# Hedgehog attention into an ELU MLP on one core: MLP chunks cut along the batches, a ring for the transposed activations, some PSUM copies on the other engine, and a new written-out order

## The chip, the core and the metric

The kernel runs on one core of a Trainium2 chip. The core has a matrix engine (TensorE; "PE" in the profile, its weight loads "PEld"), a vector engine (VectorE, "DVE"), an activation engine (ScalarE, "ACT"), a general-purpose engine (GpSimd, "POOL") and a queue engine (SyncE, "SP"). Each engine works through its own instruction list in order and waits on semaphores for the others. The metric is the device time of one execution in microseconds (us); lower is better.

## What is computed

Inputs are q, k and v of shape 8 x 8 x 576 x 64 (batch, head, position, head dimension), a feature matrix w_phi of 64 x 128, and two MLP weights of 512 x 2048 and 2048 x 512. All are float32.

```python
def phi(x):
    proj = einsum('bhsd,df->bhsf', x, w_phi)
    proj = proj - max(abs(proj), axis=-1, keepdims=True)
    return concatenate([exp(proj), exp(-proj)], axis=-1)
q_p, k_p = phi(q), phi(k)
kv  = einsum('bhsf,bhsd->bhfd', k_p, v)
z   = sum(k_p, axis=2)
num = einsum('bhsf,bhfd->bhsd', q_p, kv)
den = einsum('bhsf,bhf->bhs', q_p, z)[..., None] + 1e-06
x   = (num / den).transpose(0, 2, 1, 3).reshape(4608, 512)
h   = x @ w_in
g   = where(h > 0, h, exp(min(h, 0)) - 1)
out = g @ w_out                      # 4608 x 512, float32
```

So a linear attention with an exponential feature map feeds an MLP with the ELU function. The attention has no softmax over positions; its per-row maximum is taken over the 128 features.

## The kernel before

**Attention, by groups.** Four heads (two pairs) of one batch make a group; there are NG = 16 groups, two for each batch, numbered n. Positions are cut into nine slots of 64, and a tile of 128 rows holds one slot of two heads, or two slots of one head. A group goes through these steps, each named by a letter in the order string:

- e, f, g (L189): load k, q and v of a batch by DMAs that the POOL queue issues and that cast to bf16. h and i load w_in (two halves) and w_out the same way.
- j/k and l/m (L207, L219): PE transposes and VectorE copies of k and q for groups 0 to 3. n and o (L225): DMA transposes on the SP queue for groups 4 to 15.
- A, B, C (L233, L247, L254): k times w_phi, two exponentials on ScalarE (128 x 768 each), row maxima on VectorE. D, E, F: the exponential of the maxima, and v scaled by it on POOL (L275).
- M, N (L287, L303): q times w_phi and its row maxima. O (L317): the maxima split into two bf16 parts, 128 x 18, by a cast and a subtraction; P (L333): a PE transpose of them; Q (L338): its copy from PSUM (128 x 128).
- S, T (L343, L390): the projection of q with the maximum subtracted by a second matmul, and two exponentials.
- U, V (L401, L417): k_p times v, accumulated over the nine slots, and its copy from PSUM (128 x 520).
- W, X (L430, L448): q_p times kv, and the division on VectorE. The result goes, transposed, into `xT_sb`, by PE and copies (Y, Z) for groups 0 and 1 and by SP's DMA transposes (z, L490) for the others.

**MLP, by chunks.** The 4608 tokens are cut into nine chunks of 512 columns of `xT_sb`, one constant tile that holds all tokens. p (L507): for each of 16 blocks of d_ff, four matmuls of 512 columns (in chunk 0, two halves of 256 columns). q, r, s (L519 to L533): exponential on ScalarE, clamp on POOL, and the ELU result on VectorE. t (L535): the second product, four times four matmuls for each of four token tiles; u (L546): its copy from PSUM on ScalarE (128 x 512, float32), v (L550): two stores. In `xT_sb` the columns of a batch pair stand as 512 (slots 0 to 7 of the first batch), 128 (slot 8 of both), 512 (slots 0 to 7 of the second). The nine chunks therefore run across batch boundaries.

**What sets the order.** Nothing is scheduled by a framework: all pools stand in one manual schedule, and the string `ORDER` lists 1737 steps. A letter calls the next step of its kind, and a digit names the PSUM bank that the step writes:

```python
for letter, bank in re.findall(r"([A-Za-z])(\d?)", "".join(ORDER.split())):
    fn, args = queues[letter]
    fn(*next(args), **({"bank": int(bank)} if bank else {}))
```

Each engine's instruction list is the order of the string with the other engines' steps left out. A step is on a fixed engine; only `m_split` (O) chooses, POOL for groups below `PE_TRANSPOSED` = 4 and VectorE otherwise:

```python
eng = nc.gpsimd if n < PE_TRANSPOSED else nc.vector
```

The MLP steps of a chunk are interleaved with the attention steps of later groups.

Of the kernel before, what the change touches and what calls it, by code (L numbers as in the profile page):

```python
# [18 lines left out]
eabefegcj7dfkA0gj7BfkBeA2CA4hBl7gl6Bmj1mj0hBCM6iBkkA2DCBFEl1NDA4Bl0EmBOCFP1BEA6QBmS2CEM0CTU4eNDB  # L19
EUTOEM6VM0DP3NW4EQNM6S2NM0OTFENU6TXP1FOUQS2VP5Y4Tj1ZS6QTl0W4mTS2kTj0XTW6TkS4XA0Tj3BY2ZA6Tkl2Bp3m  # L20
Y5BCqBZrA0p4sCM2qp5rNM6qDrBNp3l2sqp7BmrsqM4rp6NFp2qsqrp5srp4CqOqrP7l3srW0sgQmp6sEj7XqS2DTrEkM0p5
NY7qTsrS0sFp4EZTsM2M6TNp5EqNS0qrp3Trp2sOsTA6fp4CqU0qrrUBssVqA2Bp5rW0sBP7p6Xqnt4qrBrsp1QCp5zqp7qr
sp0qrszW2DsrqFsS5rEp1sTXp7qp0Trfsp3qA1rtBesqp7ECoqp6qtDrBrsp5rzsqEp0sqS1qztTrrsFTsp7EU5uS1qrUrTs
A3Vt0TCtsBW1oW5BXp7A3qtCzrtsBXzt7BnM1A5M3NBtuCztDFNEM0BztNgM2uvt6ODENP7M0nM4QNES2tTNFTfS0S4TEA2t
CTp7TTU0UBA4VtBCp1qorBW2sqp0vBOXrp7quP5p4rzQsDqFW2sqrzp6XrA0qEp5szBsp3rqCvp7rqseBp4vsrqp6DsrqS0s
rM2Tp5NFEqp7sqrp3qrsTp4rsqsM0qA5rt2CEp7NBrtsBsM0qS5NtrTEsTS0U3oTA5UCTtVBt7OnBP4W0QuS3XvW5TtDXzTE
tztfFA0EuzS2M4Bt6NTztCTS4BM2otDTEtzTFA0Eut7CntNgBA4BM2CtNtBBA0OU2CUDuP6p5VQM2qM6Np4rNEp3qBsW6rqp
2sBrp5XqFeW0qsrzS6DXrp4TEzTp3sqEsvM0S6Np2TFnEqS0Tp5rqrsU6qzrUsTrp4TzOsp3qVorA0qsA6p2Brsvsp5qCP4r
p3qQCBrp4qsW0qrst2DXBEp5BFsW0zrqtEszXS6rtTvsM0A3NtBnTt5CztDBFEM0S6zNM3TtENTU0guA3S6UTotVBvt2BtTC
p1OA3qW6urp0XBP5tBQztqCzS5uA3t7DCTEntsDBFtrBEsW1TtXEA3uM5ep0NzBEp7Cqvp6rBFsM1qp5NqrM3qrS0Np2Trsf  # L30
# [15 lines left out]
def kernel(  # L46
# [34 lines left out]

    consts = ctx.enter_context(tc.tile_pool(name="consts", bufs=1))
# [5 lines left out]
    moep = ctx.enter_context(tc.tile_pool(name="moep", bufs=2))  # L88
    epool = ctx.enter_context(tc.tile_pool(name="epool", bufs=4))
# [24 lines left out]
    xT_sb = consts.tile([P, N_CT, NTOK], BF16)  # L114
    FULL = 4 * P

    def full_col(b):
        return (b // 2) * 2 * S + (b % 2) * (FULL + P)

    def mixed_col(b):  # L120
        return (b // 2) * 2 * S + FULL + (b % 2) * D

    def out_rows(tile_index):
        bp, t = divmod(tile_index, 9)
        rows = []
        for half in range(2):
            if t == 4:
                b, s = 2 * bp + half, 8
            else:
                b, t4 = (2 * bp, t) if t < 4 else (2 * bp + 1, t - 5)  # L130
                s = 4 * (t4 // 2) + t4 % 2 + 2 * half
            rows.append(
                out[b * S:(b + 1) * S, :].rearrange("(p s) c -> s p c", s=NS)[s]
            )
        return rows
# [11 lines left out]
    PIECES = (((0, 4), (4, 7), (7, 9)), ((0, 3), (3, 6), (6, 9)))  # L147
    TILES = (
# [56 lines left out]


# [12 lines left out]
    def t_copy(name, n, j0, j1):  # L219
        nc.vector.tensor_copy(  # L220
            get((name + "T", n), new_t(name))[:, j0:j1, :],
            st["tr", name, n, j0][:, 0:j1 - j0, :],
        )

    def t_dma(name, n):  # L225
        nat = st[name, n // 2][:, 2 * (n % 2):2 * (n % 2) + 2]
        nc.sync.dma_start_transpose(
            out=get((name + "T", n), new_t(name)),
            in_=nat.rearrange("p r s d -> p (r s d)"),
        )  # L230
# [56 lines left out]
    def m_mm(n, c, bank=None):  # L287
        own = min(n // FIRST, 1)
# [14 lines left out]
    def m_max(n, c):  # L303
        p0, p1 = PIECES[min(n // FIRST, 1)][c]
# [12 lines left out]
    def m_split(n, part):  # L317
# [5 lines left out]
        if n < FIRST and part == 0:  # L323
            mq, eng = st["mq0", n], nc.vector
        else:
            mq = st["mq", n][:, :, p[0]:p[1]]
            eng = nc.gpsimd if n < PE_TRANSPOSED else nc.vector
# [10 lines left out]
    def m_copy(n, part):  # L338
        st["mT", n] = tpool.tile([P, 1, P], BF16, name="mT")
        nc.vector.tensor_copy(st["mT", n], st["trm", n][:, 0:1, :])  # L340


    def q_mm(n, c, bank=None):  # L343
# [3 lines left out]
        qT, mT = st["qT", n], st["mT", n]  # L347
# [17 lines left out]
        for x in range(max(len(r) for r in runs)):  # L365
            for par in range(2):
                if x >= len(runs[par]):
# [6 lines left out]
                    qT[rows, i:i + m, :].rearrange("p i (h t) -> p h i t", h=2),  # L374
                    start=(x == 0),
                    stop=False,
                )
        for j in range(w):
            for par in range(2):
# [4 lines left out]
                    mT[rows, 0, :],  # L384
# [32 lines left out]
    def kv_copy(n):  # L417
        st["kv", n] = work.tile([P, 2, 2, 2, D + 1], BF16, name="kv_sb")
        nc.vector.tensor_copy(
# [10 lines left out]
    def x_mm(n, part, bank=None):  # L430
        Eq, kv_sb = st["Eq", n], st["kv", n]
        parts = x_parts(n, part)
# [30 lines left out]

    def x_pe(n, part, bank=None):
# [8 lines left out]
    def x_copy(n, part):  # L473
# [3 lines left out]
        c0 = full_col(b) + part * 2 * P  # L477
        nc.vector.tensor_copy(
            xT_sb[:, 2 * g:2 * g + 2, c0:c0 + 2 * P].rearrange(
# [4 lines left out]
        if part == 1:  # L484
            nc.vector.tensor_copy(
                xT_sb[:, 2 * g:2 * g + 2, mixed_col(b):mixed_col(b) + D],
                tr[:, :, 2, D:P],
            )

    def x_dma(n, pr, mixed):  # L490
        b, g = divmod(n, 2)
        xp, ct = st["xp", n, pr], 2 * g + pr
        if not mixed:
            nc.sync.dma_start_transpose(
                out=xT_sb[:, ct, full_col(b):full_col(b) + FULL].rearrange(
# [4 lines left out]
        else:  # L500
            nc.sync.dma_start_transpose(
                out=xT_sb[:, ct, mixed_col(b):mixed_col(b) + D].unsqueeze(1),
# [4 lines left out]
    def h_mm(ch, jt, h0, h1, bank=None):  # L507
        ph = psum[:, bank, h0:h1]
        for ct in range(N_CT):
# [3 lines left out]
                xT_sb[:, ct, ch * CHUNK + h0:ch * CHUNK + h1],  # L513
# [32 lines left out]
    def o_copy(ch, tt):  # L546
        st["o", ch, tt] = opool.tile([P, DM], FP32, name="o_sb")
        nc.scalar.copy(st["o", ch, tt], st["po", ch, tt])  # L548

    def o_store(ch, tt):  # L550
        last = (ch, tt) == o_tiles[-1]
        for half, rows in enumerate(out_rows(ch * (CHUNK // P) + tt)):
            queue = nc.scalar if last and half == 0 else nc.sync
            queue.dma_start(out=rows, in_=st["o", ch, tt][half * D:(half + 1) * D])

# [17 lines left out]
    def blocks(name, n):  # L573
# [3 lines left out]
    m_parts = groups((0,), first=EACH)  # L577
# [31 lines left out]
        W=(x_mm, groups(*PAIR, first=EACH)), X=(x_div, groups(*PAIR, first=EACH)),  # L609
# [9 lines left out]
    for letter, bank in re.findall(r"([A-Za-z])(\d?)", "".join(ORDER.split())):  # L619
        fn, args = queues[letter]  # L620
        fn(*next(args), **({"bank": int(bank)} if bank else {}))
    assert all(next(args, None) is None for _, args in queues.values())

# [29 lines left out]
```

## Time and profile before

| what | value |
|---|---|
| median of 3 runs | 378.05 us (377.97 to 380.45) |
| the profiled execution, its own time | 379.34 us |
| its span, first to last instruction | 377.5 us |
| TensorE busy | 349.3 us, 93% of the span |
| VectorE busy | 249.0 us, 66% |
| ScalarE busy | 248.3 us, 66% |
| GpSimd busy | 192.3 us, 51% |
| mean granted TensorE clock | 0.991 |
| data moved by DMA | 39.72 MB |

The page of a profile gives for each engine its busy time, then the span in 40 equal slices with a digit for the busy tenths, then the chain of work that ended last, then groups of equal instructions with count, total and mean duration and the idle time ahead of them. Durations of neighbouring instructions on one engine overlap a little, so a sum of means is some per cent above the busy time. A matmul's end is modelled; its starts and those of the weight loads are recorded.

### The profile page before, as it was taken

How to read it: one execution, taken by the hardware profiler on the slowest of the kernel's cores; microseconds unless marked ns; L12 is line 12 of the kernel's file. 1: busy time of each engine (PE TensorE's matmuls, PEld its weight loads, DVE VectorE, ACT ScalarE, POOL GpSimd, SP SyncE). 2: the span in 40 equal slices, each digit the busy share in tenths (PEclk: the TensorE clock that was granted, in tenths of full speed). 3: DMA queues.
4: the chain of work that ended last, by engine and by line, in shares of the span. 5: the costliest groups of instructions: out<-in, count | busy, mean ns of one | idle time of the engine just before them, and what ended most of it. 6: DMA issues, size and time to landing. Idle time of an engine off the chain costs nothing.

```text
span 377.5 us, 9991 instructions
## 1 busy us (share of the span) xinstructions
PE 349.3 (93%) x4034; PEld 193.1 (51%) x4084; DVE 249.0 (66%) x441; ACT 248.3 (66%) x453; POOL 192.3 (51%) x301
## 2 busy tenths in 40 slices
PE   2777899969999999999999999999999999999995
PEld 1665676625455555544655544644555444444442
DVE  3988986794984789658868687748754473523320
ACT  3867688648887698678965898298666453514521
POOL 8851869261954396528563575518552363413310
PEclk9899999998999999999999999999999999999999
DMA  7999988799558967478984991733014300123213
GB/s 115 202 212 209 207 124 130 96 152 141 102 77 131 157 113 104 95 137 136 151 128 94 184 168 38 118 76 76 2 23 84 76 13 0 36 50 76 63 38 76
DMA packets 68158, 39.72 MB, mean 105 GB/s; under 512 B 48016, under 2 KB 62480, under 8 KB 68112
## 3 DMA queue, kind: packets, MB, share of 16 engines
q0 software_dynamic: 15856, 18.35, 31.9%
q1 hardware_dynamic: 52176, 20.59, 31.4%
q8 instruction: 32, 0.52, 0.6%
q10 hardware_dynamic: 80, 0.13, 0.1%
q14 instruction: 14, 0.11, 0.1%
HBM read 36.77 MB, written 9.44 MB: 122 GB/s over the span
## 4 chain that ended last, share of the span: by engine, by line
PE 81%; DVE 7%; POOL 5%; issue 4%; ACT 1%; DMA 1%; SPq 0%; POOLq 0%; ACTq 0%; DVEq 0%
PE banks L538 31%; PE banks L510 30%; PE banks L439 5%; PE banks L409 5%; PE banks L238 3%; PE banks L371 3%; POOL e_sb L526 2%; PE banks L294 2%; DVE mq L312 2%; PE banks L381 2%; POOL vs L275 2%; DVE mk L256 1%; DVE mhl L328 1%; DMA e_sb<-in_w_phi_dram 1%; DVE gT L530 1%
## 5 line engine op out<-in xcount | busy, mean ns | idle before, releaser
L526 POOL TENSOR_SCALAR e_sb<-e_sb 128x512 f32<-128x512 f32 (+1 forms) x160 | 90.0, 570 | 126.1 <-ACT e_sb L521 118.9
L510 PE MATMUL banks<-xT_sb,w_in_sb 128*128 128x512 bf16 (+1 forms) x620 | 137.4, 357 | 2.2 <-issue 0.6
L538 PE MATMUL banks<-w_out_sb,gT 128*128 128x512 bf16 x546 | 133.2, 381 | 3.3 <-issue 2.4
L530 DVE SCALAR_TENSOR_TENSOR gT<-e_sb,banks 128x512 bf16<-128x512 f32 (+1 forms) x160 | 96.7, 630 | 48.8 <-POOL e_sb L526 48.3
L521 ACT ACTIVATE e_sb<-banks 128x512 f32<-128x512 f32 (+1 forms) x160 | 87.2, 561 | 48.9 <-PE banks L510 41.9
L249 ACT ACTIVATE EK<-banks 128x768 bf16<-128x768 f32 x96 | 75.1, 813 | 22.2 <-PE banks L238 14.7
L393 ACT ACTIVATE Eq<-banks 128x768 bf16<-128x768 f32 (+2 forms) x96 | 73.9, 815 | 23.6 <-PE banks L381 22.9
L510 PEld LDWEIGHTS <-w_in_sb 128*128 128x128 bf16 x640 | 58.8, 98 | 59.5 <-issue 2.3
L275 POOL TENSOR_TENSOR vs<-vn,em 128x576 bf16<-128x576 bf16 x64 | 73.2, 1153 | 23.0 <-ACT em L266 22.7
L538 PEld LDWEIGHTS <-gT 128*128 128x128 bf16 x576 | 52.7, 98 | 60.4 <-issue 0.7
L256 DVE TENSOR_REDUCE mk<-banks 128x6 f32<-128x768 f32 x48 | 45.7, 954 | 15.3 <-PE banks L238 8.0
L312 DVE TENSOR_REDUCE mq<-banks 128x6 f32<-128x768 f32 (+1 forms) x46 | 42.5, 941 | 11.9 <-PE banks L294 10.2
L548 ACT COPY o_sb<-banks 128x512 f32<-128x512 f32 x36 | 21.0, 591 | 25.8 <-PE banks L538 18.9
L456 DVE TENSOR_TENSOR xp<-banks,rec 128x640 bf16<-128x640 f32 (+2 forms) x32 | 26.4, 824 | 1.1
L439 PEld LDWEIGHTS <-Eq 128*128 128x128 bf16 x640 | 23.7, 97 | 6.1 <-issue 0.9
L439 PE MATMUL banks<-kv_sb,Eq 128*128 128x65 bf16 x640 | 25.1, 194 | 0.3 <-DVE mq L312 0.2
L409 PE MATMUL banks<-vs,EK 64*128 64x65 bf16 x1152 | 23.2, 194 | 1.0 <-DVE mq L312 0.6
L409 PEld LDWEIGHTS <-EK 64*128 64x128 bf16 x1152 | 21.0, 96 | 4.1 <-issue 1.7
L238 PE MATMUL banks<-w_sb,kT 64*128 64x128 bf16 x288 | 16.6, 225 | 4.0 <-DVE kT L220 2.4
L294 PE MATMUL banks<-w_sb,qT 64*128 64x128 bf16 x288 | 16.4, 223 | 1.3 <-DVE xp L456 0.7
L371 PE MATMUL banks<-qT,w_sb 64*128 64x384 bf16 (+2 forms) x102 | 16.6, 331 | 0.9 <-DVE mq L312 0.4
L381 PE MATMUL banks<-mT,sel 64*128 64x128 bf16 x288 | 16.6, 223 | 0.0
(45 smaller groups left out, 157.2 us busy)
## 6 DMA issues: line engine op xcount, KB each, us to landing
out_dram<-o_sb SPq DMA_DIRECT2D x71, 128.0 KB, 2.5
qn<-in_q_dram POOLq DMA_DIRECT2D x7, 576.0 KB, 7.2
kn<-in_k_dram POOLq DMA_DIRECT2D x7, 576.0 KB, 7.8
vn<-in_v_dram POOLq DMA_DIRECT2D x7, 576.0 KB, 6.8
w_in_sb<-in_moe_w_in_dram POOLq DMA_DIRECT2D x2, 1024.0 KB, 20.2
w_out_sb<-in_moe_w_out_dram POOLq DMA_DIRECT2D x1, 2048.0 KB, 32.2
xT_sb<-xp SPq DMA_TRANSPOSE x56, 2.4
qn<-in_q_dram POOLq DMA_DIRECT2D x2, 288.0 KB, 6.1
```

The source lines that it names most:

```text
L249: nc.scalar.activation(EK[:, sg, 6 * c:6 * c + 6, :].rearrange("p (i r) f -> p r i f", r=2), st["pk", n, c], ACT.Exp, scale=1.0 - 2.0 * sg,)
L256: nc.vector.tensor_reduce(mk[:, 6 * c:6 * c + 6].rearrange("p (i r) -> p r i", r=2), st["pk", n, c], axis=AX.X, op=ALU.max, apply_absolute ...
L275: nc.gpsimd.tensor_tensor(get(("vs", n), new_vs)[:, sg, r, 0:D], st["v", n // 2][:, 2 * (n % 2) + pr], st["em", n][:, sg, r].unsqueeze(2). ...
L312: nc.vector.tensor_reduce(mq, st["pm", n, c][:, :, 0:p1 - p0, :], axis=AX.X, op=ALU.max, apply_absolute_value=True,)
L393: nc.scalar.activation(Eq[:, sg, :, :, p0 * D:p1 * D].rearrange("p h r x -> p r h x"), st["pq", n, c][:, :, 0:(p1 - p0) * P].rearrange("p ...
L409: nc.tensor.matmul(kv[:, hi, pr, sg, :], EK[rows, sg, pr * NS + s, :], vs[rows, sg, pr * NS + s, :], start=(s == 0), stop=(s == NS - 1),)
L439: nc.tensor.matmul(pn[:, hi, x, :], Eq[:, sg, hi, par, i0 * D:(i0 + 2) * D], kv_sb[:, hi, pr, sg, :], start=(sg == 0), stop=(sg == 1),)
L510: nc.tensor.matmul(ph, w_in_sb[:, ct, jt * P:(jt + 1) * P], xT_sb[:, ct, ch * CHUNK + h0:ch * CHUNK + h1], start=(ct == 0), stop=(ct == N_ ...
L521: nc.scalar.activation(e_sb, st["ph", ch, jt, h0], ACT.Exp)
L526: nc.gpsimd.tensor_scalar(e_sb, e_sb, 1.0, 0.0, op0=ALU.min, op1=ALU.max)
L530: nc.vector.scalar_tensor_tensor(gT[:, jt, h0:h1], st["e", ch, jt, h0], -1.0, st["ph", ch, jt, h0], op0=ALU.add, op1=ALU.max,)
L538: nc.tensor.matmul(po, st["gT", ch][:, jt, tt * P:(tt + 1) * P], w_out_sb[:, jt, :], start=(jt == 0), stop=(jt == N_JT - 1),)
```

## The change

Four things are changed.

1. **Chunks follow the batches.** Chunk b, for b from 0 to 7, is slots 0 to 7 of batch b; chunk 8 holds slot 8 of all eight batches. `out_rows` gives the rows of `out` to match.
2. **A ring.** In place of `xT_sb` for all tokens there is a pool of four buffers of 512 columns, and a constant tile `xT_last` for chunk 8.
3. **A star in the order.** A letter followed by `*` calls its step with `other=True`. Copies k, m, Q, V and Z then go to ScalarE, u goes to VectorE, and O goes to the engine that it otherwise does not use. The new order has 47 stars: u 15, Q 11, V 10, O 7, m 2, k 1, Z 1.
4. **A new order** of the same 1737 steps, with the same number of each letter.

The diff also brings code for groups from `JOINED` on (a form of the maxima and the division without the second matmul). `JOINED` is 16 and there are 16 groups, numbered 0 to 15, so none of its branches is taken and its steps (w, x, R, y) have no instances.

```diff
-    xT_sb = consts.tile([P, N_CT, NTOK], BF16)
-    FULL = 4 * P
-    def full_col(b):
-        return (b // 2) * 2 * S + (b % 2) * (FULL + P)
-    def mixed_col(b):
-        return (b // 2) * 2 * S + FULL + (b % 2) * D
+    RING = 4
+    xtp = ctx.enter_context(tc.tile_pool(name="xtp", bufs=RING))
+    xT_last = consts.tile([P, N_CT, CHUNK], BF16)
+    def xT_of(ch):
+        if ch == N_CHUNK - 1:
+            return xT_last
+        return get(("xT", ch), lambda: xtp.tile([P, N_CT, CHUNK], BF16, name="xT"))
...
-            if t == 4:
-                b, s = 2 * bp + half, 8
+            if ch == N_CHUNK - 1:
+                b, s = 2 * t + half, 8
             else:
-                b, t4 = (2 * bp, t) if t < 4 else (2 * bp + 1, t - 5)
-                s = 4 * (t4 // 2) + t4 % 2 + 2 * half
+                b, s = ch, 4 * (t // 2) + t % 2 + 2 * half
...
+    def copy_on(scalar):
+        return nc.scalar.copy if scalar else nc.vector.tensor_copy
...
-    def t_copy(name, n, j0, j1):
-        nc.vector.tensor_copy(
+    def t_copy(name, n, j0, j1, other=False):
+        copy_on(other)(
...
-            eng = nc.gpsimd if n < PE_TRANSPOSED else nc.vector
+            eng = nc.gpsimd if (n < PE_TRANSPOSED) != other else nc.vector
...
-        nc.vector.tensor_copy(st["mT", n], st["trm", n][:, 0:1, :])
+        copy_on(other)(st["mT", n], st["trm", n][:, 0:1, :])
...
-    def kv_copy(n):
+    def kv_copy(n, other=False):
         st["kv", n] = work.tile([P, 2, 2, 2, D + 1], BF16, name="kv_sb")
-        nc.vector.tensor_copy(
+        copy_on(other)(
...
-                xT_sb[:, ct, ch * CHUNK + h0:ch * CHUNK + h1],
+                xT_of(ch)[:, ct, h0:h1],
...
-    def o_copy(ch, tt):
+    def o_copy(ch, tt, other=False):
         st["o", ch, tt] = opool.tile([P, DM], FP32, name="o_sb")
-        nc.scalar.copy(st["o", ch, tt], st["po", ch, tt])
+        copy_on(not other)(st["o", ch, tt], st["po", ch, tt])
...
-    for letter, bank in re.findall(r"([A-Za-z])(\d?)", "".join(ORDER.split())):
+    for letter, star, bank in re.findall(r"([A-Za-z])(\*?)(\d?)", "".join(ORDER.split())):
         fn, args = queues[letter]
-        fn(*next(args), **({"bank": int(bank)} if bank else {}))
+        how = {"bank": int(bank)} if bank else {}
+        if star:
+            how["other"] = True
+        fn(*next(args), **how)
```

The two orders begin like this (before, then after):

```
eabefegcj7dfkA0gj7BfkBeA2CA4hBl7gl6Bmj1mj0hBCM6iBkkA2DCBFEl1NDA4Bl0EmBOCFP1BEA6QBmS2CEM0CTU4eNDB
...
eabeefgcj7dj6fkA0gk*CeA2A4CBj7CBl6Dkj1Bml0kDA6mEBM0CBA2ENBEBCl5l4BfmOBmhP7A0QM4BFES6NDBM2ETOCP5E
```

## The prediction

> **What bounds the kernel now.** First the page: who is busy, and when.
>
> ```profile
> PE 349.3 (93%) x4034; PEld 193.1 (51%) x4084; DVE 249.0 (66%) x441; ACT 248.3 (66%) x453; POOL 192.3 (51%) x301
> ...
> PE   2777899969999999999999999999999999999995
> ...
> DVE  3988986794984789658868687748754473523320
> ACT  3867688648887698678965898298666453514521
> ...
> PEclk9899999998999999999999999999999999999999
> ```
>
> TensorE is full from the tenth slice (9.44 us each) to the end. It is short of work in the first five slices and once in the ninth. The clock has two dips, in slices 2 and 9. So I asked for the stages by their busy time (columns: length, then busy us and count of PE, PEld, DVE, ACT, POOL, then the clock):
>
> ```profile
> 0.00:33.00 33.00, 20.78 (x413) 16.36 (x414) 24.00 (x51) 21.01 (x35) 21.45 (x36) 0.95 1.06 181
> 33.00:52.00 19.00, 15.82 (x257) 11.54 (x255) 17.77 (x38) 14.10 (x33) 13.00 (x28) 1.00 1.12 181
> 52.00:78.00 26.00, 25.18 (x333) 16.43 (x336) 19.27 (x40) 19.54 (x41) 14.24 (x28) 1.00 0.82 121
> 78.00:90.00 12.00, 8.81 (x143) 4.84 (x143) 7.66 (x8) 6.69 (x12) 5.00 (x6) 0.86 1.32 153
> 90.00:373.00 283.00, 278.67 (x2902) 143.92 (x2939) 180.26 (x307) 186.49 (x335) 138.55 (x205) 1.00 0.52 89
> 373.00:377.50 4.50, 0.00 (x0) 0.00 (x0) 0.00 (x0) 0.48 (x1) 0.00 (x0) 1.00 0.22 58
> ```
>
> Of TensorE's 28.2 idle us, 12.2 lie before 33 us, 3.2 in 33 to 52, 0.8 in 52 to 78, 3.2 in 78 to 90, 4.3 spread over the next 283, and 4.5 are the last copy and store. From 90 us on nothing but fewer or cheaper matmuls could help. In 33 to 52 VectorE is 94% busy and is the limit. The hole at 78 has one cause, which the instructions in order of time show:
>
> ```profile
> 78.60 3.23 DVE L328 CAST mhl<-mq 128x18 bf16<-128x18 f32 x1
> 78.70 2.27 POOL L275 TENSOR_TENSOR vs<-vn,em 128x576 bf16<-128x576 bf16 x2
> ...
> 80.91 0.26 POOL L284 CAST vs<-em 128x18 bf16<-128x18 f32 x1
> 81.04 0.80 POOL L192 DMA_DIRECT2D qn<-in_q_dram  x1
> ...
> 82.10 0.23 PE L335 MATMUL banks<-ident,mhl 128*128 128x128 bf16 x1 [2.62 <-DVE mhl L329]
> ```
>
> with, from the answer for line 328,
>
> ```profile
> L328 DVE CAST mhl<-mq x12: 168/180/3226, 78.6 to 274.5; 128x18 bf16<-128x18 f32 x12
> ```
>
> A cast that takes 0.18 us eleven times took 3.23 once: it ended as POOL's run of back-to-back work did (81.83 and 81.84). TensorE waited 2.62 us for it, and the clock view then has 3.41 us at half speed (83.92 to 87.33), which loses 1.7 more. The event costs 4.3 us.
>
> **The change, part by part.**
>
> *Chunks and ring.* The program has as many matmuls as before, of the same sizes: no gain there. Chunk ch could start after batch min(ch, 7) before, and can only then now. The ring's fifth batch writes its buffer while the order has long passed chunk 0's products, and no transpose in the new program has a wait on TensorE for it. Priced at 0; if that cover went, SP's transposes would wait for a chunk's sixteen blocks, 14 us. Stores have the same shape. The unused `JOINED` code costs nothing.
>
> *Order in the full stretch.* A block of four 512-column matmuls takes 0.86 us (the chain has dozens), and its first weight load stands 1.17 before the next step's when that step uses 64-row operands. The switch costs 0.3. The orders have 86 and 85 such switches: -0.3 us.
>
> *The start.* I added up, along each order, all steps ahead of the first h_mm, by their mean durations (TensorE's by the spacing of its weight loads). Before: VectorE 26.2 us, ScalarE 22.8, TensorE 19.0. The view has 24.0 busy for VectorE by 33 us (neighbours overlap, hence 0.95 of the sum), and the first h_mm at 32.4. After: VectorE 23.2, ScalarE 23.0, TensorE 18.2. VectorE loses two V (1.39), two Q (0.43), one Z (0.42), one division (1.35, moved behind) and 0.13 of k copies, and gains an m (0.42) and an O (0.36): -2.9. With 0.95 of 3.0 gone, the first h_mm comes 2.9 us earlier. TensorE has done 0.8 less by then (two A, one S), so 2.1 are gained. Bounds: 0.6, if the time goes into waiting for the projections' chain, and 3.1, if ScalarE's early k copy also shortens VectorE's own idle time. From there to the second half of chunk 0, VectorE had 21.1 us of work in 19.9 of time; now it has 18.9, but TensorE has 1.8 less to do: +-0. In the next stretch, to chunk 1, ScalarE has 27.7 for 26.0 before, against 32.9 for TensorE: no limit.
>
> *Loads.* POOL now issues w_in's second half at some 23 us instead of 10, and w_out behind the second clamp, at some 34 instead of 11.6. From 14 to 46 us the traffic of before is flat at 0.207 MB a us. w_out is 2.1 MB in bf16: 10.1 us, so about 46 with landing. Its first product stands at 38.1 us of TensorE's sum, where before it stood at 39.0 and came at 53.9; less 0.9 and the 2.1 gained, that is 50.9. The cover is 5 us; past it, each us late is a us. v of batch 2 is issued 7.2 us of TensorE's work before its use, where a landing takes 6.8, and U follows 3.8 later. Both at 0; bound +3.
>
> *The stars.*
>
> ```profile
> L548 ACT COPY o_sb<-banks 128x512 f32<-128x512 f32 x36 | 21.0, 591 | 25.8 <-PE banks L538 18.9 <-DMA out_dram<-o_sb 4.6 <-ACT Eq L393 2.2
> ...
> L419 DVE CAST kv_sb<-banks 128x520 bf16<-128x520 f32 x16 | 11.1, 696 | 7.1 <-PE banks L409 6.8
> ...
> L340 DVE COPY mT<-banks 128x128 bf16<-128x128 bf16 x18 | 3.9, 218 | 3.6 <-PE banks L335 3.6
> ```
>
> No row has V or Q on ScalarE. V's nearest is L548, a copy of the same width: 0.59. Q lies on the line through the 256- and 512-column exponentials (0.391, 0.604): 0.29. u on VectorE is nearest to L419: 0.68. The Trainium skill's page "ScalarE: Activation LUTs", section "Rules for kernel authors", speaks against moving copies there: plain arithmetic belongs on VectorE, up to about three times faster per element in bf16. By that, V would take up to 2.1 us and its ten moves would cost 14 us of ScalarE's time. The rows say otherwise for float32 from PSUM: 0.59 against 0.70. I take the row. ScalarE then gets 10 x 0.59 + 11 x 0.29 + 2.7 (k, m, Z) = 11.8 and gives 15 x 0.59 = 8.9: +2.9, at 66% busy. VectorE gives 7.0 + 2.4 + 1.9 + 1.8 (five O to POOL) and gets 10.2 and two O: -2.2. In the full stretch both are covered by TensorE's 98%.
>
> What can reach TensorE is latency. U's product waits for V, W waits for it. In the new order TensorE has 1.03 us of other work between U and W at the closest place and 1.19 at the next three, against 0.59 plus two hand-overs of about 0.1. A moved copy that finds an exponential (0.81) just begun misses this by 0.6; on average by 0.2. Five such places make 1.0; for the P-Q-S chain (closest 0.86) I add 0.5. So +1.5, bounds 0 and the second rival's.
>
> *The hole at 78.* Group 4's O is starred: it goes to POOL, where the same two instructions take 0.20 + 0.22 and cannot be held by POOL. The event goes, -4.3. What is late next there: M's last part to P has 4.7 us of TensorE work for 0.95 + 0.42, so nothing. Seven O of groups 7, 8 and 10 to 14 stay on VectorE. How long can one be held? The skill's page "SBUF — State Buffer", section "Who interferes with whom", says that a VectorE copy in a two-port mode and a GpSimd instruction exclude each other, the second waiting "for the whole instruction". That is one POOL instruction, 1.15 us at most, and nothing would show at P. The row says 3.05 us, through four POOL instructions in a row. By the row, and with 1 of 12 held before, seven O bring 0.6 such events; but the seven have at least 4.2 us between M and P, and need 1.7. A hold of 3.05 then costs about 0.5. Counted in the +1.5.
>
> **The sum.** -2.1 - 0.3 - 4.3 + 1.5 = -5.2. On the profiled execution, 379.3 becomes 374.1; its span is 377.5. The median run is 1.3 lower: 378.05 - 5.2 = 372.9, so 373.
>
> **The rivals.**
>
> *The hole moves.* For it: the hole is one chance meeting of two engines, and a new order brings new meetings: O of group 12 beside the load of k, O of group 7 right behind two v steps. Against: the slack between M and P. Then -2.1 - 0.3 + 1.5 = -0.9: 377.
>
> *ScalarE's queue.* V and Q stand behind exponentials in a list that is worked in order, and W, S and all TensorE work behind them wait. If each of the 21 moved copies is late by a whole exponential less its 0.2 of slack, 0.6 each, it is 12.6 in place of 1.5: 378 - 6.7 + 12.6 = 384. It decides from 0.32 us a place on (6.7 / 21). For it: between the first and the ninth h_mm of the new order ScalarE has 10.7 us of work against TensorE's 7.8. Against: 66% busy over the whole, and only five places that are tight.
>
> *The weights come late.* If w_out's issue slips behind clamps that wait for ScalarE by 6 to 10 us, TensorE stands 2 to 6 at its first product, and a stop of that size brings half-clock time again: 376 to 382.
>
> **How the numbers follow.** Forecast 0.55 (369 to 375.5), hole moves 0.22 (375 to 379.5), ScalarE's queue 0.17 (378 to 388), late weights 0.06. About 1% (3.8 us) is what a measurement tells from no change. Faster than 374.3: nine tenths of the forecast, 0.49. Slower than 381.8: 0.12 of the queue and 0.04 of the weights and of what I overlooked, 0.16. The rest, 0.35, is within 1%. The range leaves out 0.05 below 369 and 0.15 above 381.
>
> **What will show it.** Right: the first h_mm near 29.5 us; VectorE under 90% in the stretch after it; no O above 0.5 us near group 4; one half-clock window, in the start, not two; TensorE still idle for 4 to 6 us in the 283 that follow; V on ScalarE near 0.59. Wrong: waits of weight loads of L439 or L371 on ScalarE's kv_sb or mT above 3 us together; a wait of L538 on w_out's landing; a stop of TensorE over 1.5 us after 60 us with the clock at half behind it.

## The result and the profile after

The changed kernel takes 373.21 us (median of 4 runs, 372.49 to 373.53); the kernel before took 378.9 beside it (4 runs, 377.97 to 380.45). The ratio is 0.9843, with a 95% interval of 0.9801 to 0.9886: about 5.7 us faster. (Ratios leave out executions that took over 1.5% more than the fastest of their kernel; there are such in experiments 5, 7, 9 and 10 alone, and the medians given there are those of all executions.) The profiled execution took 373.46 us with a span of 371.7; before it was 379.34 and 377.5.

The page of the changed kernel, the rows that answer to those of before:

```profile
PE 349.8 (94%) x4034; PEld 193.6 (52%) x4084; DVE 244.7 (66%) x425; ACT 251.5 (68%) x463; POOL 194.3 (52%) x307
...
PE   2798799999999999999999999999999999999994
...
PEclk9999999999999999999999999999999999999998
```

TensorE's busy time is what it was (349.8 for 349.3), so the gain is idle time that went: 28.2 us before, 21.9 after. (Work at half speed counts as busy, so what the clock costs lies inside the busy time.) VectorE lost 4.3 us, 3.05 of them the held cast, and ScalarE got 3.2 (the sum had -2.2 and +2.9). The dip in the ninth slice and the second dip of the clock are gone. By stages (length, then busy us and count of PE, PEld, DVE, ACT and POOL, clock, DMA share, GB/s):

```profile
0.00:30.00 30.00, 20.35 (x358) 15.82 (x358) 19.89 (x42) 19.38 (x34) 19.33 (x32) 1.00 1.01 167
30.00:50.00 20.00, 17.17 (x266) 12.54 (x265) 18.31 (x37) 17.54 (x40) 13.34 (x26) 1.00 0.96 156
50.00:75.00 25.00, 24.47 (x386) 16.14 (x384) 19.48 (x43) 20.03 (x42) 13.32 (x26) 1.00 0.87 137
75.00:90.00 15.00, 14.73 (x212) 8.27 (x210) 10.21 (x17) 12.11 (x25) 10.75 (x18) 1.00 0.96 154
90.00:366.50 276.50, 272.54 (x2833) 140.82 (x2874) 176.82 (x288) 181.82 (x326) 137.60 (x207) 1.00 0.55 92
```

From 75 to 90 us TensorE stands 0.3 us, where before it stood 3.2 between 78 and 90. In the long stretch it stands 4.0 us of 276.5 (before: 4.3 of 283). The start is still the largest loss, some 10 us.

Three of the operations that changed their engine (V at L487, Q at L406, u at L671; min/median/max in ns):

```profile
L487 ACT CAST kv_sb<-banks x10: 592/592/600, 21.8 to 239.6; 128x520 bf16<-128x520 f32 x10
...
L406 ACT COPY mT<-banks x11: 259/266/306, 19.1 to 272.5; 128x128 bf16<-128x128 bf16 x11
...
L671 DVE COPY o_sb<-banks x15: 678/684/692, 62.2 to 363.6; 128x512 f32<-128x512 f32 x15
```

They were taken at 0.59, 0.29 and 0.68 us from the nearest rows of before, and come at 0.592, 0.266 and 0.684.

**Where the time went.** To compare two orders I use one figure at a few places of the program: the time at which a step's first weight load starts, less the 4.6 us ahead of the first matmul, less 0.961 times the sum of the durations of all TensorE steps that the order puts ahead of it. It is the time that TensorE has lost so far, idle or at half speed, up to a constant that cancels in differences; a falling value only means that the following steps overlap better than 0.961. Within one order two rows differ by measured times alone. Between the two orders the difference is an estimate, since other steps stand ahead of the same place.

| lost up to | first h_mm (L633) | second half of chunk 0 | chunk 1 | chunk 2 | last matmul |
|---|---|---|---|---|---|
| before | 9.6 (at 32.4 us) | 12.2 | 16.0 | 14.8 | 14.0 |
| after | 9.5 (at 31.5 us) | 11.3 | 9.3 | 8.1 | 8.6 |
| after's code, before's order (experiment 1) | 10.4 | 13.0 | 16.7 | 15.5 | 14.7 |
| before, O on GpSimd (experiment 2) | 10.4 | 13.0 | 12.3 | 11.7 | 10.9 |
| after, no stars (experiment 3) | 10.4 | 13.2 | 11.4 | 11.7 | 15.4 |
| after, O without stars (experiment 4) | 9.6 | 11.1 | 9.1 | 8.0 | 8.5 |
| after, V and Q without stars (experiment 5) | 10.4 | 12.4 | 10.6 | 9.7 | 11.7 |

Between before and after the last column differs by 5.4; what is left to the 5.8 us by which TensorE's end moved (372.8 to 367.0), some 0.5, is a difference of the two orders' sums of durations. With a second set of durations (each step's spacing by its own kind and that of the step behind it, after 55 us) such differences come out up to 0.6 us larger or smaller.

### The profile page after: what moved, and what is told of

Its sections match the earlier page's. It is cut to its first block, busy times and chain, and to the rows that moved or that the text cites. A ratio compares the mean times of both kernels' runs of the same rounds, so it can differ in the third digit from the quotient of the medians.

```text
span 371.7 us, 9982 instructions
## 1 busy us (share of the span) xinstructions
PE 349.8 (94%) x4034; PEld 193.6 (52%) x4084; DVE 244.7 (66%) x425; ACT 251.5 (68%) x463; POOL 194.3 (52%) x307
## 4 chain that ended last, share of the span: by engine, by line
PE 82%; DVE 7%; ACT 3%; issue 3%; POOL 2%; DMA 1%; POOLq 0%; ACTq 0%
PE banks L661 32%; PE banks L633 29%; PE banks L477 5%; PE banks L526 5%; PE banks L437 3%; PE banks L341 2%; PE banks L267 2%; PE banks L449 2%; ACT EK L278 2%; DVE gT L653 2%; POOL e_sb L649 1%; DVE mk L285 1%; DMA kn<-in_k_dram 1%; DVE xp L543 1%; DVE mq L368 1%
## 5 line engine op out<-in xcount | busy, mean ns | idle before, releaser
L661 PE MATMUL banks<-w_out_sb,gT 128*128 128x512 bf16 x549 | 134.8, 379 | 2.6 <-issue 1.9
L653 DVE SCALAR_TENSOR_TENSOR gT<-e_sb,banks 128x512 bf16<-128x512 f32 (+1 forms) x160 | 98.3, 630 | 53.0 <-POOL e_sb L649 52.3
L633 PE MATMUL banks<-xT,w_in_sb 128*128 128x512 bf16 (+1 forms) x554 | 124.0, 355 | 1.7 <-issue 0.3
L633 PEld LDWEIGHTS <-w_in_sb 128*128 128x128 bf16 x640 | 58.3, 98 | 57.2 <-issue 0.6
L461 ACT ACTIVATE Eq<-banks 128x768 bf16<-128x768 f32 (+2 forms) x96 | 74.1, 815 | 14.8 <-PE banks L449 13.5
L671 ACT COPY o_sb<-banks 128x512 f32<-128x512 f32 x21 | 12.3, 585 | 17.4 <-PE banks L661 16.6
L671 DVE COPY o_sb<-banks 128x512 f32<-128x512 f32 x15 | 10.3, 685 | 14.3 <-DMA out_dram<-o_sb 10.1
L341 PE MATMUL banks<-w_sb,qT 64*128 64x128 bf16 x288 | 16.7, 225 | 1.9 <-DVE gT L653 1.3
## 6 DMA issues: line engine op xcount, KB each, us to landing
w_in_sb<-in_moe_w_in_dram POOLq DMA_DIRECT2D x2, 1024.0 KB, 10.6
w_out_sb<-in_moe_w_out_dram POOLq DMA_DIRECT2D x1, 2048.0 KB, 15.6
```

What stands on the lines that cost most here:

```text
L461: nc.scalar.activation(Eq[:, sg, :, :, p0 * D:p1 * D].rearrange("p h r x -> p r h x"), st["pq", n, c][:, :, 0:(p1 - p0) * P].rearrange("p ...
L633: nc.tensor.matmul(ph, w_in_sb[:, ct, jt * P:(jt + 1) * P], xT_of(ch)[:, ct, h0:h1], start=(ct == 0), stop=(ct == N_CT - 1),)
L653: nc.vector.scalar_tensor_tensor(gT[:, jt, h0:h1], st["e", ch, jt, h0], -1.0, st["ph", ch, jt, h0], op0=ALU.add, op1=ALU.max,)
L661: nc.tensor.matmul(po, st["gT", ch][:, jt, tt * P:(tt + 1) * P], w_out_sb[:, jt, :], start=(jt == 0), stop=(jt == N_JT - 1),)
```

## The experiments

Each run had runs of the kernel before beside it, whose medians lay between 379.14 and 379.73. Experiments 1 to 4 ran beside the same ones, 5 to 8 likewise, and so on in pairs. The changed kernel was not run again beside them: a comparison with its 373.21 us is one across sittings, in which the kernel before moved by 0.8 (378.9 to 379.7).

### 1. The new code with the old order

```diff
 ORDER = """
-eabeefgcj7dj6fkA0gk*CeA2A4CBj7CBl6Dkj1Bml0kDA6mEBM0CBA2ENBEBCl5l4BfmOBmhP7A0QM4BFES6NDBM2ETOCP5E
+eabefegcj7dfkA0gj7BfkBeA2CA4hBl7gl6Bmj1mj0hBCM6iBkkA2DCBFEl1NDA4Bl0EmBOCFP1BEA6QBmS2CEM0CTU4eNDB
...
```

> The chunks that follow the batches and the ring of four, with the old order and no stars. Theory (order and engines make the gain): same as before, within 1 us, and the 3 us cast at group 4 with its half-clock window is still there. Rival (layout or the ring moves time): 3 us or more either way.

379.23 us (10 runs, 378.12 to 381.49), ratio 0.9985 [0.9963, 1.0008]. The chunks along the batches and the ring bring and cost nothing that is clear of noise. The held cast is there again, in order of time:

```profile
79.39 3.23 DVE L393 CAST mhl<-mq 128x18 bf16<-128x18 f32 x1
79.49 2.27 POOL L303 TENSOR_TENSOR vs<-vn,em 128x576 bf16<-128x576 bf16 x2
...
82.89 0.23 PE L400 MATMUL banks<-ident,mhl 128*128 128x128 bf16 x1 [2.62 <-DVE mhl L394]
```

The same 3.23 us as before the change (3226 and 3228 ns), the same 2.62 us of TensorE, and 3.41 us of half clock from 83.6 on: it came in both profiled executions of the old order, and in none of the new one.

### 2. The kernel before, with every O on GpSimd

```diff
-            eng = nc.gpsimd if n < PE_TRANSPOSED else nc.vector
+            eng = nc.gpsimd
```

> The kernel before, with the split of the row maxima on GpSimd for every group and nothing else changed. Theory (the held cast at group 4 is worth its wait and the half-clock time behind it): about 4 us faster than before, no split instruction above 0.5 us, no half-clock window near 84 us. Rival (the hole is a mark of one execution, or the time is lost again at the next wait): within 1 us of before.

(Another branch keeps the first parts of groups 0 and 1 on VectorE.) 375.9 us (374.46 to 376.8), ratio 0.9894 [0.9858, 0.9929]. The cast's line, and two of the stages that were shown of before:

```profile
L328 POOL CAST mhl<-mq x16: 189/205/217, 22.8 to 270.6; 128x18 bf16<-128x18 f32 x14, 128x10 bf16<-128x10 f32 x2
```

```profile
52.00:78.00 26.00, 24.76 (x354) 16.40 (x350) 19.25 (x41) 19.84 (x43) 13.80 (x28) 1.00 0.79 115
78.00:90.00 12.00, 11.19 (x180) 6.32 (x180) 7.86 (x12) 8.90 (x16) 7.21 (x13) 1.00 1.08 168
```

No cast above 0.22 us, TensorE busy 11.19 us where it was 8.81, the clock at 1.00 for 0.86. Against experiment 1, whose start lost the same to 0.02 us, it has lost 4.4 us less at chunk 1 and 3.9 less at the end. One line of code takes away the hole, at the price that was put on it (4.3).

### 3. The new order without its stars

All 47 stars go; one line of the twenty that have some:

```diff
-W0eqZp5sFrsP7p4EqXQ*qS2rTsrS0sfM6Tsp5NETY4p3ZqEA6Tp2Cp4qrqU0BrsrsUqsBp5rVeS2qst7TrTA0p6CW2qsp4rB
+W0eqZp5sFrsP7p4EqXQqS2rTsrS0sfM6Tsp5NETY4p3ZqEA6Tp2Cp4qrqU0BrsrsUqsBp5rVeS2qst7TrTA0p6CW2qsp4rB
...
```

> The changed kernel with every starred step back on its old engine; order and layout stay. Theory (the order was laid out for the stars; the early copies and the split count most): 2 to 6 us slower than the changed kernel, lost before 90 us. Rival (the stars do nothing, the order alone has the gain): within 1 us of the changed kernel.

380.1 us (379.31 to 380.91), ratio 1.0008 [0.9992, 1.0025]. All of the gain is gone, but not where I had put it:

```profile
L394 DVE CAST mhl<-mq x12: 168/180/993, 77.7 to 274.3; 128x18 bf16<-128x18 f32 x12
```

Group 4's O is on VectorE again, and no cast is held longer than 0.99 us; TensorE has lost 5.3 us less at chunk 1 than in experiment 1. So the new order takes the hole away without the star. What is lost instead comes later, in a drip: 4.0 us between chunk 1 and the end, where with the stars the figure falls by 0.7. Among TensorE's waits from 78 us on are these:

```profile
PE banks L526 <- DVE kv_sb L487: 1.0, 2, 0.8
PE banks L526 <- DVE xp L543: 0.4, 1, 0.4
PE banks L437 <- DVE mT L406: 0.3, 1, 0.3
```

(Columns: the waiting engine and what it waited for, us in total, times, longest.) kv_sb and mT are copies that the stars had moved; xp is a division, on VectorE with the stars too. In the changed kernel the same rows of TensorE's matmuls name no other engine. The waits that name kv_sb or mT come to about 1.5 of the 4.0 us; the rest carries no name. Stars with the old order were not run.

### 4. to 7. The stars by kind

One kind of star is taken away in each, with one line of the order shown: O (4), V and Q (5), u (6), k, m and Z (7).

```diff
-Q*TNU4FDFM6UBENj3V*S0kFEW4Tj7XU2hTUgkM4V*Y6NOM0Z*P7W2QNS4l7O*TXP6S0Q*Tl6mY3j2TZS4Tkj7mTW2kTp7XS0
+Q*TNU4FDFM6UBENj3V*S0kFEW4Tj7XU2hTUgkM4V*Y6NOM0Z*P7W2QNS4l7OTXP6S0Q*Tl6mY3j2TZS4Tkj7mTW2kTp7XS0
...
```

> The changed kernel with only the seven stars on the split of the row maxima taken off, so that groups 4, 5, 6, 9 and 15 split on VectorE again. Theory (VectorE's small cast can be held by GpSimd's run of work, wherever they meet): one or more splits above 1 us, and 0 to 4 us slower than the changed kernel, most if group 4's is held. Rival (the new order keeps them apart by itself): no split above 0.5 us, same time.

373.31 us (372.92 to 374.06), ratio 0.9837 [0.9816, 0.9858]: the same as the changed kernel.

```profile
L394 DVE CAST mhl<-mq x12: 168/178/724, 75.5 to 269.4; 128x18 bf16<-128x18 f32 x12
```

The longest cast is 0.72 us, and TensorE's loss is within 0.2 us of the changed kernel's at every place of the table. The stars of O bring nothing measurable in this order.

```diff
-Q*TNU4FDFM6UBENj3V*S0kFEW4Tj7XU2hTUgkM4V*Y6NOM0Z*P7W2QNS4l7O*TXP6S0Q*Tl6mY3j2TZS4Tkj7mTW2kTp7XS0
+QTNU4FDFM6UBENj3VS0kFEW4Tj7XU2hTUgkM4VY6NOM0Z*P7W2QNS4l7O*TXP6S0QTl6mY3j2TZS4Tkj7mTW2kTp7XS0
...
```

> The changed kernel with the 21 stars on V (128x520 copy) and Q (128x128 copy) taken off, so these copies are on VectorE again. Theory (the moved V and Q are what the new order needs, since VectorE is behind where they stand): most of the 6.8 us that all stars are worth, 3 to 6 us slower than the changed kernel, with waits for kv_sb and mT. Rival (ScalarE's queue delays them, as the prediction's second rival has it): the same time or faster than the changed kernel.

377.23 us (10 runs, 376.05 to 384.24, four of them above 381), ratio 0.9951 [0.9917, 0.9986]. Its profiled execution, 376.55, has lost 0.9 at the first h_mm, 1.2 at chunk 1 and 3.1 at the end more than after. By this trace and the ratios V and Q on ScalarE are worth 3 to 4 us, the most of any kind of star, from the start to the end of the attention. What those four lost is not in a trace.

```diff
-TW0QTt7XDBEW5zBS0XEtTzTA2S5CtTzu*BtTS0u*t4ToBM5tNTA2nM5BtNDBM0EA5tBCFp7EuNBU2FqOA0CUBnrp4VDzCM5q
+TW0QTt7XDBEW5zBS0XEtTzTA2S5CtTzuBtTS0ut4ToBM5tNTA2nM5BtNDBM0EA5tBCFp7EuNBU2FqOA0CUBnrp4VDzCM5q
...
```

> The changed kernel with the 15 stars on u taken off, so that all 36 output copies are on ScalarE. Theory (u was moved to make room on ScalarE for V and Q): 1 to 3 us slower than the changed kernel, ScalarE 3 points busier. Rival (ScalarE has room for all): within 0.5 us.

374.81 us (374.04 to 375.45), ratio 0.9881 [0.9854, 0.9908]: 1.6 slower. The trace has lost 0.4 less than after at the first h_mm and 1.4 more at the end, so the loss lies behind chunk 1, where ScalarE has V, Q and now every u.

```diff
-eabeefgcj7dj6fkA0gk*CeA2A4CBj7CBl6Dkj1Bml0kDA6mEBM0CBA2ENBEBCl5l4BfmOBmhP7A0QM4BFES6NDBM2ETOCP5E
+eabeefgcj7dj6fkA0gkCeA2A4CBj7CBl6Dkj1Bml0kDA6mEBM0CBA2ENBEBCl5l4BfmOBmhP7A0QM4BFES6NDBM2ETOCP5E
...
```

> The changed kernel with the four stars on k, m and Z taken off: all transposed copies of groups 0 to 3 on VectorE. Theory (VectorE limits the start): 1 to 2 us slower, all of it lost before 50 us. Rival (the start is limited by loads and by the cold clock): within 0.5 us.

375.75 us (10 runs, 373.12 to 380.52, two of them above 380), ratio 0.9894 [0.9859, 0.993]. The trace has lost 0.2 more at the first h_mm and 0.5 at chunk 1; that much belongs to these four stars. The rest of this execution's excess lies at one stop far from them:

```profile
189.39 0.84 POOL L201 DMA_DIRECT2D vn<-in_v_dram  x1
189.40 1.36 SPq L251 DMA_TRANSPOSE qT<-qn  x1
...
198.77 0.50 PE L341 MATMUL banks<-w_sb,qT 64*128 64x128 bf16 x6 [2.58 <-DMA qT<-qn]
```

with the clock at half from 198.4 to 201.8 us. It is the same chain of events as before's at 78 us: a stop of some 2.6 us, then one window of 3.41 us at half speed. The transpose that TensorE waited for left together with a load of v and landed 9.3 us later. In the changed kernel the same two leave together, and the transpose takes 5.8; experiments 9 and 10 have more such cases. Why it took 3.5 us longer here isn't shown, so the four stars are worth between 0.5 and 2.5 us.

### 8. A warmed-up TensorE

The prediction had the first h_mm at 29.5 us, and it came at 31.5. One suspect is the clock in the start, so eight matmuls on zeros go ahead of it, whose result nobody reads.

```diff
+        warm = consts.tile([P, 512], BF16, name="warm")
+        nc.vector.memset(warm, 0.0)
+        for _ in range(8):
+            nc.tensor.matmul(psum[:, 5, :], warm[:, 0:P], warm, start=True, stop=True)
```

> The changed kernel with eight 512-column matmuls on zeros ahead of all TensorE work, while it waits for the first load; their result is not read. Theory (the half clock of the first 24 us is what ate the start's expected 2 us): a full-speed window before 10 us and 1 to 2 us faster than the changed kernel. Rival (VectorE sets the start, TensorE's speed does not matter there, or the clock falls back because early work is sparse): within 0.5 us.

374.91 us (373.54 to 375.89), ratio 0.9873 [0.9838, 0.9907]: no gain, and 1.7 above the changed kernel's median. The full clock came at 4.0 us for one window, fell back, came again for one window at 14.2, and stayed only from 24.4 on, where it came to stay in the changed kernel too (24.7). TensorE was busy for 1.5 us in each of the two windows of 3.4. Chunk 1 began 0.5 us earlier all the same, and then TensorE stood 2.6 us between 78 and 96 us, where it stands 0.2 in the changed kernel. In the order of time:

```profile
80.26 2.26 POOL L308 TENSOR_TENSOR vs<-vn,em 128x576 bf16<-128x576 bf16 x2 [4.18 <-DMA vn<-in_v_dram]
...
94.01 0.69 DVE L675 COPY o_sb<-banks 128x512 f32<-128x512 f32 x1 [2.26 <-DMA out_dram<-o_sb]
...
94.75 2.53 PE L637 MATMUL banks<-xT,w_in_sb 128*128 128x512 bf16 x11 [1.50 <-DVE o_sb L675]
```

GpSimd waits 4.2 us for v of batch 2, VectorE stands behind the store of output tile 0, and TensorE behind VectorE. Experiments 9 to 12 ask whether these transfers are what the new order now lacks.

### 9. and 10. Three transfers earlier, without and with the warm-up

The loads of v (g) and q (f) and the store (v) each go to an earlier place:

```diff
-stO*qXDrp6Bp5qsP1zW2qQrrsp4FsS0qXnp6Trp5EqzA2TtCrqEp1sDp0sBFtroEsBS4u*qp6EqTp7zU2TrrsUqsnqS4rV*r
-p1ssW2zqTt7rsXop6A0qtTCrzM2sBW4NztBXp6M0qM2zA4NrtBgst1BNutCM2A6DM4NBFtO*fNBP3tQ*CM4S2t0u*TNTp7ED
+stO*qXDrp6Bp5qsP1zW2qQrrsgp4FsS0qXnp6Trp5EqzA2TtCrqEp1sDp0sBFtroEsBS4u*qfp6EqTp7zU2TrrsUqsnqS4rV
+*rp1ssW2zqTt7rsXvop6A0qtTCrzM2sBW4NztBXp6M0qM2zA4NrtBst1BNutCM2A6DM4NBFtO*NBP3tQ*CM4S2t0u*TNTp7E
...
```

> The changed kernel with three transfers issued earlier in the order and nothing else changed: v of batch 2 and q of batch 3 some 8 us earlier, and the store of output tile 0 ahead of q's transposes of group 5 on SP's queue. If what still stands between 78 and 96 us in the changed kernel is waiting for these transfers (GpSimd waited 2.41 us for v of batch 2), the wait of GpSimd at 79 us is gone, VectorE doesn't wait for the store of tile 0, and the time is 0.5 to 1.5 us below the changed kernel, about 372.3. If those waits are covered by queued work of TensorE, the wait is gone from GpSimd's row and the time stays within 0.5 us of 373.2.

> The same three moves together with the warm-up of the run before (eight products of zeros, whose result nobody reads). If late transfers are what ate the warm-up's gain of 0.5 us at the start of chunk 1, this ends 0.5 to 1 us below the kernel with the moves alone, and 3 us below the warm-up without them (374.9). If the warm-up gains nothing by itself, the two kernels with the moves agree within 0.5 us.

None of the expectations held: 380.81 us (12 runs, 374.24 to 381.63), ratio 0.9923 [0.9881, 0.9965], and, with the warm-up, 379.49 (10 runs, 374.17 to 381.78), ratio 0.9939 [0.9895, 0.9983]. Of the 22 executions 17 took 378 us or more and lost most or all that the change had won; the other five lie at 374.2 to 375.5. SP's first transposes of groups 4 and 5 in the changed kernel:

```profile
57.94 2.19 SPq L251 DMA_TRANSPOSE kT<-kn  x1
...
64.19 1.32 SPq L251 DMA_TRANSPOSE kT<-kn  x1
```

and in experiment 10 (379.36 us), first on SP's queue and then on TensorE:

```profile
59.53 2.99 SPq L255 DMA_TRANSPOSE kT<-kn  x1
...
64.01 2.91 SPq L255 DMA_TRANSPOSE qT<-qn  x1
...
69.23 3.91 SPq L255 DMA_TRANSPOSE kT<-kn  x1
```

```profile
73.82 0.47 PE L345 MATMUL banks<-w_sb,qT 64*128 64x128 bf16 x6 [3.34 <-DMA qT<-qn]
```

The issue of a transpose takes 2.9 to 3.9 us instead of 1.3 to 2.2, and group 4's qT lands 9.8 us from its issue instead of 3.3. The queues from 62 to 68 us, in the changed kernel and in experiment 10 (packets, MB, and the time of the packets as a share of that of 16 DMA engines):

```profile
q1 hardware_dynamic: 3008, 0.74, 83.6%
```

```profile
q1 hardware_dynamic: 1377, 0.33, 73.0%
q0 software_dynamic: 426, 0.47, 51.2%
```

q1 is SP's queue, and q0 has GpSimd's loads, 576 KB each; none runs in the changed kernel in these 6 us. By the byte, SP's packets took twice as long beside the loads (73.0% for 0.33 MB, 83.6% for 0.74). TensorE then stood 3.3 us for qT, and its clock was at half for 3.41 us after. It is no matter of this place alone: in the fourteen traces together the 144 transposes of k and q with no load in flight landed in 3.2 to 5.6 us (median 3.4), and the 107 that had one in flight for over half of their time in 3.2 to 11.8 (median 6.5). The changed kernel has them too (10.3 us for qT from 133.0 on), where TensorE's work covers them.

### 11. and 12. The store alone earlier, without and with the warm-up

Of the three moves only that of v stays:

```diff
-p1ssW2zqTt7rsXop6A0qtTCrzM2sBW4NztBXp6M0qM2zA4NrtBgst1BNutCM2A6DM4NBFtO*fNBP3tQ*CM4S2t0u*TNTp7ED
-S1qEA3S5TCtrTtEsToBU1FEp7TvBgA5UCqnO*p4V*rBW1szDp3qXvrtqsBW1rEp7sXp6qEA3u*qM1rnp5Brsp0qszBp7rNqp
+p1ssW2zqTt7rsXvop6A0qtTCrzM2sBW4NztBXp6M0qM2zA4NrtBgst1BNutCM2A6DM4NBFtO*fNBP3tQ*CM4S2t0u*TNTp7E
+DS1qEA3S5TCtrTtEsToBU1FEp7TBgA5UCqnO*p4V*rBW1szDp3qXvrtqsBW1rEp7sXp6qEA3u*qM1rnp5Brsp0qszBp7rNqp
```

> The changed kernel with only the third of the three moves: the store of output tile 0 goes ahead of q's transposes of group 5 on SP's queue; the loads of v and q stay where the change put them. In the run with all three moves the transposes of group 4 took 3.3 to 4.0 us each where the changed kernel's took 1.3 to 2.2, TensorE stopped 3.7 us for qT and the clock was halved for 6.8 us. If the two loads did that, by moving their bytes while those transposes ran, this kernel has neither and lies within 0.6 us of 373.2. If the store is what hurts, as a write in among the transposes, it stays near 379.

> The early store together with the warm-up of eight products of zeros. In the warm-up run alone VectorE stood 2.26 us behind that store at 94 us and TensorE 1.5 us behind VectorE. If this is what ate the warm-up's gain, the time is 0.5 to 1 us below the early store alone, about 372.5, and below the changed kernel. If the wait for v of batch 2 at 80 us is enough to eat it, it stays at 374 to 375.

374.0 us (6 runs, 372.59 to 375.68), ratio 0.9872 [0.9846, 0.9897], and 373.63 (5 runs, 371.92 to 374.26), ratio 0.9853 [0.9831, 0.9876]. The first lies 0.8 from the changed kernel's median, a little beyond the 0.6 expected, and none of these 11 executions is above 375.68, where 17 of the 22 with the loads moved took 378 or more. So the store alone does no such harm, and the loads are needed for it; the loads without the store, and each load alone, were not run. GpSimd's wait for v of batch 2 is still there (2.71 us at 78.9 us), and TensorE has no wait on another engine from 75 to 100 us. The second has in its trace what was hoped for: no wait of VectorE on that store, 1.1 us less lost than in experiment 11 at chunk 1 and 1.8 less at the end, and with 371.92 the shortest execution of all. But its median is 0.4 above the changed kernel's, and the ranges of the three kernels lie over each other. No version is shown to be faster than the change.

## Why the prediction held, and which step failed

The forecast was 373 and the time is 373.21. By its steps:

| step | in the sum | by the table above | by the second set of durations |
|---|---|---|---|
| start, to the first h_mm | -2.1 | -0.1 (-0.9 against experiment 1) | -0.5 (-1.3) |
| from there to the second half of chunk 0 | 0 | -0.9 | -0.9 |
| hole at 78, to chunk 1 | -4.3 | -5.7 | -5.3 |
| small waits of the moved copies, to the end | +1.5 | +1.3 | +0.7 |
| the order's own sum (forecast: switches) | -0.3 | -0.5 | +0.2 |
| sum | -5.2 | -5.8 | -5.8 |

The last row of the forecast is not borne out: of the 86 and 85 switches 75 lie behind the first h_mm in both orders, so none is saved in the full stretch, where the term was put. That the total hit within 0.4 us is in part luck. The start fell short by 1.2 to 2.0 us, and the stretch behind it and the hole gave some 2 us more than they were priced at.

**The hole** was right in place and size. Experiment 2 takes it away alone, for 4.4 us at chunk 1 and 3.9 at the end, and experiment 1 has it back with 3228 ns for 3226. The step's reason was half wrong: "Group 4's O is starred: it goes to POOL" would remove it, but it isn't needed. Without the star (experiment 4) group 4's cast took 0.17 us at its new place in the order. Nor was "1 of 12 held before" right. A minimum, a median and a maximum hide the others: three more of before's twelve took 0.55 to 0.82 us. In the traces of all fourteen programs 26 of these casts took longer than 0.22 us, and each ended within 0.05 us of the end of a GpSimd instruction: 23 behind one instruction, as the prediction quotes of the page, one behind two, and the two of 3.23 us behind four in a row. What decides how many isn't shown. After the change the longest is 0.31 us, so the seven O that stayed cost nothing:

```profile
L394 DVE CAST mhl<-mq x9: 170/174/310, 28.0 to 252.2; 128x18 bf16<-128x18 f32 x8, 128x10 bf16<-128x10 f32 x1
```

What this stretch gained beyond experiment 2's 4.4 us, about 1 us, is left to the order by subtraction; no run separates it.

**The start failed.** The step was "With 0.95 of 3.0 gone, the first h_mm comes 2.9 us earlier"; it came 0.9 earlier. It took VectorE as the only limit and put TensorE's half speed in the start at nothing. The work did leave VectorE: 21.3 us busy by the first h_mm, where it was 23.5. But it waited for 10.2 us instead of 8.9. Two stages of the changed kernel, cut where before's clock rose for good and where its own did,

```profile
19.06:24.70 5.64, 5.45 (x114) 4.55 (x113) 2.75 (x5) 3.94 (x8) 5.51 (x10) 1.00 1.15 211
24.70:31.52 6.82, 6.56 (x176) 5.30 (x175) 6.11 (x16) 5.34 (x10) 0.18 (x1) 1.00 1.12 204
```

and the first of them in the kernel before:

```profile
19.06:24.70 5.64, 4.25 (x139) 3.36 (x135) 5.29 (x13) 2.96 (x5) 4.79 (x10) 1.00 1.13 210
```

show TensorE full and VectorE half idle after the change; before, VectorE was full (5.29 us) and TensorE was not (4.25). (The clock column has no record of the changed kernel ahead of 24.7 us and prints 1.00.) TensorE was at half speed there for the most part, as the weight loads of U say (129 ns against 94, medians), in this stage and right after it; before's had a median of 95 in this stage:

```profile
L477 PEld LDWEIGHTS <-EK x72: 100/129/148, 19.0 to 21.5; 64*128 64x128 bf16 x72
...
L477 PEld LDWEIGHTS <-EK x60: 92/94/96, 24.9 to 25.9; 64*128 64x128 bf16 x60
```

5.45 us at half speed is up to 2.7 us more than at full (an estimate), the size of what is missing. Nor is before's early rise at 19.1 us the rule: in experiments 1 and 2, with the old start, the full clock came to stay at 22.2 and 28.1 us, and in the ten other traces of the new order it came at 22.2 to 26.1. Against experiment 1, the new start brings 0.9 to 1.3 us rather than 0.1 to 0.5.

The traces also show what the time of this rise is worth. In the old order it moved the first h_mm little: 32.4, 33.2 and 33.2 us for rises at 19.1, 22.2 and 28.1 (before, experiments 1 and 2). In the eight traces of the new order with the stars of its start in place (all but experiments 3, 5 and 7; in 4 an O differs) the first h_mm goes with it, from 30.4 us for a rise at 22.2 (experiment 12) to 32.8 for one at 26.1 (experiment 10; both have the warm-up), about 0.5 us for each us. So with VectorE relieved, TensorE's own speed seems to have become the limit of the start. This is a comparison of traces: no experiment sets the clock alone, and experiment 8 could not keep it high. The bound "3.1, if ScalarE's early k copy also shortens VectorE's own idle time" didn't come: the second load of k landed for TensorE only at 6.8 us, and its first product came later than before (7.4 us for 6.5).

**The loads.** "The cover is 5 us" was wrong; it was about one. From the changed kernel's instructions in order of time:

```profile
34.96 1.24 POOL L213 DMA_DIRECT2D w_out_sb<-in_moe_w_out_dram  x1
...
51.74 0.39 PE L661 MATMUL banks<-w_out_sb,gT 128*128 128x512 bf16 x1
...
79.02 1.14 POOL L304 TENSOR_TENSOR vs<-vn,em 128x576 bf16<-128x576 bf16 x1 [2.41 <-DMA vn<-in_v_dram]
```

w_out was issued at 35.0, one us behind the sum, but landed 15.6 us later, at 50.6, where the sum had 12. That the last us of cover held, and the third rival's late weights didn't come, is luck. v of batch 2 was late by 2.4 us and was covered, as the value 0 took it.

**The stars.** The rows of before were the right guide: V and Q cost 0.59 and 0.27 us on ScalarE, and their place there is worth 3 to 4 us. The Trainium skill's page "ScalarE: Activation LUTs", section "Rules for kernel authors", gives its factor for bf16, and its row names relu, max, min, add and mul. That it speaks against copies was the prediction's own reading, and so was the estimate of 2.1 us for V, which reads float32 (ten at 2.1 would be 21 us of ScalarE's time; 14 is what that is above VectorE's). The rival of ScalarE's queue had the sign the wrong way: without the stars the copies wait in VectorE's queue, and TensorE behind them, as far as the waits carry a name (experiments 3 and 5). The small waits came out at 0.7 to 1.3 for 1.5, and TensorE's idle time in the long stretch at 4.0 us. That VectorE would be under 90% busy after the start was a little off: 18.31 of 20 us.

**The rivals.** "The hole moves" didn't happen by the order; experiment 10 shows what it looks like when it does, with a stop of 3.3 us at 70 us, from another cause.

## What to carry to other kernels

Where the main engine is full, look for its few stops, price each with the half-clock time behind it, and ask which two neighbours in the order meet there: here one such meeting was worth 4 of 6 us, and another engine or another neighbour cured it alike. For a small copy, look at the queue that it stands in and at its own row on each engine: here that mattered more than either engine's load (66% before). When a relieved engine doesn't bring the time that it gave up, look which engine is full in its place, and at what clock. A load that is issued earlier to remove a covered wait runs beside something else; look first at which queue's transfers it meets.

## What was not expected of the hardware

- A held VectorE instruction is reproducible: 3226 and 3228 ns in two programs with the same order. All 26 held casts in the traces ended with a GpSimd instruction, to within 0.05 us.
- After the clock had come to stay, stops of TensorE of 2.6 to 3.3 us (before, experiments 1, 7 and 10) were each followed by 3.41 us of half clock, and one of 3.7 us (experiment 9) by 6.8; stops of up to 1.8 us (experiment 1, at 28 us) were not. The Trainium skill's page "TensorE: Matmul & The Clock Gate", Part 1, gives a window of about 3.4 us, as the records show, and a rise after one busy window. Here eight matmuls brought a rise at 4.0 to 5.6 us in all three traces that have them, and it lasted one window, in which TensorE was busy for 1.5 to 1.7 us.
- DMA transposes slowed while casting loads of 576 KB ran beside them: an issue from 1.3 to 2.2 us to 2.9 to 3.9, a landing from 3.3 us to 9.8 in experiment 10, and by the medians of all traces from 3.4 to 6.5.
